# One-core attention and gated FFN: the second exponential path as three shifted linear terms, and the FFN's gate kept in SBUF

## The chip, the cores and the metric

One core of a Trainium2 chip runs the whole program. TensorE multiplies, ScalarE evaluates exp and tanh, VectorE and GpSimd do elementwise work, SyncE issues most transfers. The time is the device time of one execution in microseconds (us); the median of the runs counts, and less is better.

## The reference

Layer norm of one sequence of 2048 tokens of width 512, then two branches on the normed tokens: attention with 32 query heads of width 16 that share one key and one value head, and a gated FFN of width 1792. The FFN's result, through a silu, scales the attention's result, and the input is added.

```python
xn = _layernorm(x, axis=-1)
q = (xn @ wq).reshape(B, S, 32, 16).transpose(0, 2, 1, 3)
k, v = xn @ wk, xn @ wv
p = _softmax(jnp.einsum("bhqd,bkd->bhqk", q, k) * 16 ** -0.5, axis=-1)
s = jnp.einsum("bhqk,bkd->bhqd", p, v).transpose(0, 2, 1, 3).reshape(B, S, 512) @ wo
b = (_silu(xn @ w_gate) * (xn @ w_up)) @ w_down
return x + s * _silu(b)
```

## The kernel before, in words

**Score tiles.** There are 1024 score tiles of 128 keys x 1024 columns (two heads x 512 queries). A block is four heads x 512 queries; it has 16 key tiles with two score tiles each, and there are 32 blocks. A score tile is two matmuls of 32 rows (L877) into one of three PSUM buffers: `ring0` and `ring1` belong to ScalarE, `ring2` to VectorE.

**Two ways to an exponential.** ScalarE reads a tile from `ring0` or `ring1` and writes exp as bf16 into one of eight buffers `Pb` (L937; the first few go to the space of `g2_sb`, shown as `g_sb`). VectorE takes the other tiles, two at a time: for each, one instruction (L997, "pass A") adds an offset to the scaled score, limits it and writes it as a 16-bit integer, whose bits, read as fp16, are a piecewise linear 2 to the power of the score. Over the pair of tiles (2048 columns) three more instructions follow: L1011 cuts out the mantissa, L1016 multiplies it with the value, and L1023 keeps the exponent. The exponent alone and the product are two terms; each is multiplied on TensorE with the value matrix scaled by its own coefficient (`VD[:, i]`), and the sum is the approximated exp times the values. All products add up in `o_ps` (L747).

**FFN.** Its 56 units (`g_ffn`) and 16 down products (`g_down`) fill TensorE's gaps. A unit multiplies the gate into `m_ps`, ScalarE takes tanh of it there (L657), VectorE makes `ab` = (tanh + 1) x gate from `th` and `m_ps` (L659), then the up product goes into the same `m_ps`, and VectorE writes `hT` = `ab` x up (L663). `m_ps` is one buffer: the up product waits for L659, the next unit for L663.

**Order.** A greedy planner in the kernel (`_Sched`, `pe_pick`, `pe_do`, `pump`) places every operation on its engine with costs written in the kernel, and the program is written out in that order; each engine then runs its own list in order. TensorE's list alternates between a *visit* to the scores (row strips: one ScalarE tile, with or without a VectorE tile behind it) and a few *groups* (four matmuls on the four column strips: products with values, FFN, projections). Where the planner sees a gap, it puts a group with zero weights (`zw`) into it. The numbers `TOL` and `MERGE` say how long TensorE may be late for, or wait for, a tile. `LOCKS` names the VectorE operations that the planner does not put beside a GpSimd operation.

Of the kernel before, what the change touches and what calls it, by code (L numbers as in the profile page):

```python
# [26 lines left out]
CE, CW = 0.66858732, 0.66372796  # L27
# [8 lines left out]
TOL, MERGE, KE, KB, KR, PW = 0.17, 0.1, 1000, 3.0, 16, 2.0  # L36
# [146 lines left out]
class _Sched:  # L183
# [4 lines left out]
    LOCKS = ("dM", "dE", "dW", "xn")  # L188
# [95 lines left out]
def kernel(  # L284
# [353 lines left out]
    def g_q(pair):
        qs, jj = pair // NQ, pair % NQ
        a = grp_pe([lambda kc=kc: cmm(m_ps, wq_sb[:, kc, jj * P:(jj + 1) * P], xnT[:, kc, qs * 512:(qs + 1) * 512],  # L640
                                      kc == 0, kc == KC - 1) for kc in range(KC)])
# [4 lines left out]

    cnt = {"f": 0}

    def g_ffn(sc, f):
# [50 lines left out]
    def g_out(n):  # L700
# [280 lines left out]
    w_ops = []  # L981

    def pool_ok(b):
        pend = sum(o.dur for o in w_ops if o.start is None)
        return cur["np"] % KE == 0 and (b > cur["ba"] or rem(b, 0) + rem(b, 1) >= KR) and max(sd.free["POOL"] - sd.free["PE"], 0.0) + pend < KB

    def dve_sc(si, b, x, start, dur):
# [27 lines left out]
        def mul(eng, a, z):  # L1015
            return lambda: eng.tensor_tensor(out=Bf[wi][:, a:z].bitcast(FP16), in0=Bf[wi][:, a:z].bitcast(FP16),  # L1016
                                             in1=U[:, a:z].bitcast(FP16), op=ALU.mult)
        if pool_ok(b):
# [390 lines left out]
```

## Time and profile before

| | |
|---|---|
| median of 3 runs | 781.51 us (780.82 to 781.6) |
| profiled execution, its span | 778.8 us |
| TensorE matmul busy | 748.9 us (96%) |
| VectorE busy | 734.0 us (94%) |
| ScalarE busy | 756.9 us (97%) |
| GpSimd busy | 54.2 us (7%) |
| granted TensorE clock, mean of the core | 0.995 |

Busy time counts an engine from the start to the end of each instruction; an instruction's end overlaps the start of the next one, so the distance from start to start, which the timeline shows, is what one costs in a row of them. The page gives the profiled execution by its span alone; the runs' median lies 2.7 us above it, which is time outside the first and last instruction.

### The profile page before, as it was taken

To read this page: it belongs to the slowest core of one execution; us is meant where nothing else is said; L and a number is where in the kernel's file an instruction comes from. 1 tells how busy PE (TensorE), PEld (TensorE's weight loads), DVE (VectorE), ACT (ScalarE), POOL (GpSimd) and SP (SyncE) were. 2 spreads that over 40 slices of the span, in tenths; PEclk is the share of its full clock that TensorE was granted. 3 is DMA by queue.
4 is the path that set the end of the run, shared out by engine and by line. 5 is a ranking of instruction groups with operands and counts; after the bars stand their busy time and mean duration, and the time that the engine had idled before them with its cause. 6 is when DMAs were issued, how large, how long until landed. Compare 5 with 4: busy or idle time off the path is not lost.

```text
span 778.8 us, 20698 instructions
## 1 busy us (share of the span) xinstructions
PE 748.9 (96%) x9093; PEld 229.7 (29%) x9095; DVE 734.0 (94%) x920; ACT 756.9 (97%) x866; POOL 54.2 (7%) x59
## 2 busy tenths in 40 slices
PE   8999999999999999999999999999999999999995
PEld 3323223322222333322233322322223233322221
DVE  7689999999999999999999999999999999999995
ACT  6999999999999999999999999999999999999993
POOL 2100000000012000000001110000000300000101
PEclk9999999999999999999999999999999999999998
DMA  9400000000001000000000100000000000000001
GB/s 327 141 9 9 16 2 24 3 8 17 4 28 50 23 2 6 18 2 24 2 10 22 49 24 2 24 1 9 16 2 24 28 23 2 2 23 3 22 2 32
DMA packets 21193, 20.15 MB, mean 26 GB/s; under 512 B 8744, under 2 KB 17192, under 8 KB 21096
## 3 DMA queue, kind: packets, MB, share of 16 engines
q1 hardware_dynamic: 19512, 18.20, 7.7%
q8 instruction: 73, 1.20, 0.6%
q10 hardware_dynamic: 1584, 0.56, 0.3%
q14 instruction: 24, 0.20, 0.1%
HBM read 14.19 MB, written 2.34 MB: 21 GB/s over the span
## 4 chain that ended last, share of the span: by engine, by line
PE 48%; ACT 45%; DVE 5%; issue 1%; SPq 0%; DMA 0%; ACTq 0%; POOL 0%; DVEq 0%; POOLq 0%
ACT Pb L937 41%; PE ring L877 17%; PE m_ps L488 16%; PE o_ps L747 13%; ACT th L657 3%; DVE Bf L997 1%; ACT g_sb L937 1%; PE ring L433 1%; DVE Bf L1016 1%; ACT th L674 1%; DVE x_sb L997 0%; DVE Bf L1023 0%; PE ring L488 0%; DVE x_sb L1016 0%; PE ring L452 0%
## 5 line engine op out<-in xcount | busy, mean ns | idle before, releaser
L937 ACT ACTIVATE Pb<-ring 128x1024 bf16<-128x1024 f32 x772 | 730.7, 1202 | 2.1 <-PE ring L877 2.1
L877 PE MATMUL ring<-QB,KT 32*128 32x512 bf16 x2048 | 306.0, 382 | 15.6 <-ACT Pb L937 9.3
L997 DVE TENSOR_SCALAR Bf<-ring 128x1024 uint16<-128x1024 f32 x172 | 209.2, 1216 | 5.2 <-PE ring L877 3.7
L877 PEld LDWEIGHTS <-KT 32*128 32x128 bf16 x2048 | 94.1, 90 | 313.9 <-issue 307.4
L747 PE MATMUL o_ps<-Pb,VA 128*32 128x512 bf16 x1544 | 146.9, 385 | 0.0
L997 DVE TENSOR_SCALAR x_sb<-ring 128x1024 uint16<-128x1024 f32 x72 | 87.6, 1217 | 2.7 <-PE ring L877 2.4
L1016 DVE TENSOR_TENSOR Bf<-Bf,Bf 128x2048 f16<-128x2048 f16 x74 | 90.0, 1216 | 0.1
L747 PE MATMUL o_ps<-xnT,zw 128*32 128x512 bf16 x1092 | 83.1, 381 | 0.0
L488 PE MATMUL m_ps<-xnT,wu_sb 128*32 128x512 bf16 x896 | 72.6, 384 | 1.1 <-DVE ab L659 1.1
L488 PE MATMUL m_ps<-wd_sb,hT 128*32 128x512 bf16 x896 | 71.5, 383 | 0.1
L488 PE MATMUL m_ps<-xnT,wg_sb 128*32 128x512 bf16 x896 | 70.4, 384 | 0.0
L747 PE MATMUL o_ps<-Bf,VD 128*32 128x512 f16 x688 | 67.1, 385 | 0.4 <-DVE Bf L1016 0.3
L732 POOL TENSOR_TENSOR oT<-oa,rb 128x512 bf16<-128x512 f32 x15 | 22.7, 1514 | 614.2 <-DMA rb<-dscr 515.7
L1023 DVE TENSOR_SCALAR Bf<-Bf 128x2048 uint16<-128x2048 uint16 x86 | 60.4, 702 | 0.6
L747 PEld LDWEIGHTS <-VA 128*32 128x32 bf16 x1560 | 38.0, 94 | 53.8 <-issue 51.5
L1011 DVE TENSOR_SCALAR Bf<-Bf 128x2048 uint16<-128x2048 uint16 x74 | 52.1, 712 | 0.0
L657 ACT ACTIVATE th<-m_ps 128x512 f32<-128x512 f32 x56 | 43.7, 781 | 0.0
L659 DVE SCALAR_TENSOR_TENSOR ab<-th,m_ps 128x512 f32<-128x512 f32 x56 | 38.1, 680 | 4.2 <-ACT th L657 3.9
L663 DVE TENSOR_TENSOR hT<-ab,m_ps 128x512 bf16<-128x512 f32 x56 | 38.1, 680 | 2.1 <-PE m_ps L488 1.7
L747 PEld LDWEIGHTS <-VD 128*32 128x32 f16 x976 | 26.6, 94 | 38.9 <-issue 35.3
L747 PEld LDWEIGHTS <-zw 128*32 128x32 bf16 x1092 | 25.8, 95 | 25.5 <-issue 12.9
L1016 DVE TENSOR_TENSOR x_sb<-x_sb 128x2048 f16<-128x2048 f16 x24 | 29.2, 1215 | 0.0
(121 smaller groups left out, 414.3 us busy)
## 6 DMA issues: line engine op xcount, KB each, us to landing
rb<-dscr SPq DMA_DIRECT2D x15, 256.0 KB
out_dram<-xn SPq DMA_DIRECT2D x16, 128.0 KB, 1.9
dn<-oa SPq DMA_DIRECT2D x120, 2.0 KB, 1.7
oa<-oa SPq DMA_DIRECT2D x60, 32.0 KB, 2.0
wg_sb<-in_B_w_gate_dram SPq DMA_DIRECT2D x1, 1792.0 KB, 12.3
wu_sb<-in_B_w_up_dram SPq DMA_DIRECT2D x1, 1792.0 KB
wd_sb<-in_B_w_down_dram SPq DMA_DIRECT2D x1, 1792.0 KB, 19.7
x_sb<-in_A_x_dram SPq DMA_DIRECT2D x3, 512.0 KB
```

The source lines that it names most:

```text
L488: return [nc.tensor.matmul(out=dst[GRP * j:GRP * j + GRP, :], lhsT=w[:, GRP * j:GRP * j + GRP], rhs=rhs, start=start, stop=stop, tile_posi ...
L657: t_ = OP("ACT", 0.477, [a], lambda: nc.scalar.activation(out=th[i][:], in_=m_ps[:], func=ACT.Tanh, scale=0.5), (0,), name="tanh")
L659: s_ = OP("DVE", 0.6, [t_, ab_rel[i]], lambda: nc.vector.scalar_tensor_tensor(out=ab[i][:], in0=th[i][:], scalar=1.0, in1=m_ps[:], op0=ALU ...
L663: h = OP("DVE", 0.6, [b], lambda: nc.vector.tensor_tensor(out=hT[:, f, :], in0=ab[i][:], in1=m_ps[:], op=ALU.mult), (1,), name="hmul")
L732: return [pk, q], lambda eng: eng.tensor_tensor(out=oT[qs % 2][:, jj, :], in0=o0[:], in1=rbt[:], op=ALU.mult)
L747: r.append(nc.tensor.matmul(out=o_ps[GRP * g:GRP * g + GRP, :], lhsT=lhs, rhs=rhs, start=(n == 0), stop=(n == pv_total[(b, g)] - 1), tile_ ...
L877: return lambda: [nc.tensor.matmul(out=ring[sl][:, u * 512:(u + 1) * 512], lhsT=KT[half][GRP * g:GRP * g + GRP, t * P:(t + 1) * P], rhs=QB ...
L937: bi = nc.scalar.activation(out=buf, in_=ring[i][:], func=ACT.Exp, scale=escale, bias=ebias)
L997: lambda: nc.vector.tensor_scalar(out=U[:, hs], in0=ring[si][:], scalar1=ubias, scalar2=UINF, op0=ALU.add, op1=ALU.min), (1.5, u), name="p ...
L1011: o1 = OP("DVE", 0.6, [pa, pa0] + wrel, lambda: nc.vector.tensor_scalar(out=Bf[wi], in0=U, scalar1=0x3FF, scalar2=0x3800, op0=ALU.bitwise_and,
L1016: return lambda: eng.tensor_tensor(out=Bf[wi][:, a:z].bitcast(FP16), in0=Bf[wi][:, a:z].bitcast(FP16), in1=U[:, a:z].bitcast(FP16), op=ALU ...
L1023: o2 = OP("DVE", 0.6, o3, lambda: nc.vector.tensor_scalar(out=U, in0=U, scalar1=0x7C00, scalar2=None, op0=ALU.bitwise_and), (2, u, 1), nam ...
```

## The change

**VectorE's path.** The split into mantissa, product and exponent is gone. The pair's integer itself is the first term; two instructions (L1020 of the changed kernel) add 683 and 341 to it and give the second and the third. Three terms with three coefficients are multiplied with the values on TensorE, and a pair takes three of the ten 2048-column buffers (it took two).

**FFN.** VectorE copies the gate from `m_ps` to `ab` (L665), ScalarE takes tanh from `ab` (L666), so the up product waits for the copy alone; VectorE makes `th` = (tanh + 1) x up (L670), and GpSimd the last product `hT` = `ab` x `th` (L673). There are two `th` buffers (one before). `hT` also takes over the space of `wk_rep` and `o_tok`, and late in the program four tiles of the input are loaded into it.

**The planner.** `MERGE` goes from 0.1 to 0.25, `LOCKS` names the shifts, and the means to give the mantissa product to GpSimd (which `KE` had switched off) go.

```diff
-CE, CW = 0.66858732, 0.66372796
+NPH = 3
+CS = (0.320556640625, 0.2021484375, 0.25439453125)
+SHIFT = (0.0, 683.0, 341.0)
...
-TOL, MERGE, KE, KB, KR, PW = 0.17, 0.1, 1000, 3.0, 16, 2.0
+TOL, MERGE = 0.17, 0.25
...
-    LOCKS = ("dM", "dE", "dW", "xn")
+    LOCKS = ("dS", "xn")
...
-        t_ = OP("ACT", 0.477, [a], lambda: nc.scalar.activation(out=th[i][:], in_=m_ps[:], func=ACT.Tanh, scale=0.5),
-                (0,), name="tanh")
-        s_ = OP("DVE", 0.6, [t_, ab_rel[i]], lambda: nc.vector.scalar_tensor_tensor(
-            out=ab[i][:], in0=th[i][:], scalar=1.0, in1=m_ps[:], op0=ALU.add, op1=ALU.mult), (1,), name="silu")
-        m_rel[0] = s_
+        s_ = OP("DVE", 0.6, [a, ab_rel[i]], lambda: nc.vector.tensor_copy(out=ab[i][:], in_=m_ps[:]), (1,), name="gev")
+        t_ = OP("ACT", 0.477, [s_, th_rel[i]], lambda: nc.scalar.activation(out=th[i][:], in_=ab[i][:], func=ACT.Tanh,
+                                                                            scale=0.5), (0,), name="tanh")
+        m_rel[:] = [s_]
         b = grp_pe([mm(wu_sb, kc) for kc in range(KC)], [ffn_in2])
-        h = OP("DVE", 0.6, [b], lambda: nc.vector.tensor_tensor(
-            out=hT[:, f, :], in0=ab[i][:], in1=m_ps[:], op=ALU.mult), (1,), name="hmul")
-        ab_rel[i] = h
-        m_rel[0] = h
+        u_ = OP("DVE", 0.6, [t_, b], lambda: nc.vector.scalar_tensor_tensor(
+            out=th[i][:], in0=th[i][:], scalar=1.0, in1=m_ps[:], op0=ALU.add, op1=ALU.mult), (1,), name="umul")
+        m_rel[:] = [u_]
+        h = OP("POOL", 1.25, [u_, s_] + hT_use(sc, f), lambda: nc.gpsimd.tensor_tensor(
+            out=hT[:, f, :], in0=ab[i][:], in1=th[i][:], op=ALU.mult), (0,), name="hmul")
+        ab_rel[i] = th_rel[i] = h
+        h_done[f] = h
...
-        o1 = OP("DVE", 0.6, [pa, pa0] + wrel, lambda: nc.vector.tensor_scalar(
-            out=Bf[wi], in0=U, scalar1=0x3FF, scalar2=0x3800, op0=ALU.bitwise_and,
-            op1=ALU.bitwise_or), (2, u, 0), name="dM")
...
-            o3 = [OP("DVE", 1.135, [o1], mul(nc.vector, 0, 2048), (2, u, 2), name="dW")]
-        o2 = OP("DVE", 0.6, o3, lambda: nc.vector.tensor_scalar(
-            out=U, in0=U, scalar1=0x7C00, scalar2=None, op0=ALU.bitwise_and), (2, u, 1), name="dE")
-        for bi, ops, vi in ((ui, [o2], 0), (wi, o3, 1)):
+        terms, rd = [(ui, [pa, pa0], 0)], []
+        for i in range(1, NPH):
+            wi, wrel = get_buf()
+            o = OP("DVE", 0.6, [pa, pa0] + wrel, lambda wi=wi, i=i: nc.vector.tensor_scalar(
+                out=Bf[wi], in0=U, scalar1=SHIFT[i], scalar2=None, op0=ALU.add), (2, u, i), name="dS")
+            rd.append(o)
+            terms.append((wi, [o], i))
+        for bi, ops, vi in terms:
```

What the planner makes of it, counted in the two built programs (for TensorE from the first to the last score tile):

| | before | changed |
|---|---|---|
| score tiles to ScalarE (exp) | 780 | 736 |
| score tiles to VectorE (pass A) | 244 | 288 |
| shifts and the like on 128x2048 | 122 L1011, 122 L1016, 122 L1023 | 288 L1020 |
| TensorE visits to the scores | 772 | 728 |
| TensorE groups of four, of them with zero weights | 1703, 270 | 1677, 85 |
| GpSimd FFN products | 0 | 56 |

In both programs every VectorE tile stands in a visit behind a ScalarE tile.

VectorE's list in the first quarter of the program, before: `Bf` and `x_sb` are the 2048-column buffers, `ring_98` is `ring2`, `m_ps` holds the FFN's gate or up product.

```order
L997 TENSOR_SCALAR x_sb<-ring_98 128x1024
L1016 TENSOR_TENSOR Bf_134<-Bf_134,Bf_133 128x2048
L642 TENSOR_SCALAR QB_120<-m_ps 128x512
L997 TENSOR_SCALAR x_sb<-ring_98 128x1024
L1023 TENSOR_SCALAR Bf_133<-Bf_133 128x2048
L1011 TENSOR_SCALAR x_sb<-Bf_135 128x2048
L997 TENSOR_SCALAR Bf_130<-ring_98 128x1024
L659 SCALAR_TENSOR_TENSOR ab_137<-th_136,m_ps 128x512
L1016 TENSOR_TENSOR x_sb<-x_sb,Bf_135 128x2048
L997 TENSOR_SCALAR Bf_130<-ring_98 128x1024
L663 TENSOR_TENSOR hT<-ab_137,m_ps 128x512
L1023 TENSOR_SCALAR Bf_135<-Bf_135 128x2048
```

About the same place of the changed program: a pass A each, and the shifts, the gate's copy and the product with tanh between them.

```order
L665 COPY ab_136<-m_ps 128x512
L1004 TENSOR_SCALAR x_sb<-ring_98 128x1024
L1020 TENSOR_SCALAR Bf_131<-Bf_129 128x2048
L1020 TENSOR_SCALAR Bf_133<-Bf_129 128x2048
L670 SCALAR_TENSOR_TENSOR th_134<-th_134,m_ps 128x512
L1004 TENSOR_SCALAR Bf_130<-ring_98 128x1024
L1020 TENSOR_SCALAR x_sb<-Bf_132 128x2048
L645 TENSOR_SCALAR QB_119<-m_ps 128x512
L1004 TENSOR_SCALAR Bf_130<-ring_98 128x1024
L1020 TENSOR_SCALAR x_sb<-Bf_132 128x2048
```

Between two passes A there stood one long and one or two short instructions; now there is one or two short ones. Behind each L670 comes a pass A or a shift: of the 56, 32 have a pass A next and 22 a shift.

GpSimd's list of the changed program, in the second FFN stretch: `oT` is the normed attention (L745, before L732) and `xn` the finished output (L708, before L695), which stood there alone before.

```order
L673 TENSOR_TENSOR hT<-ab_136,th_134 128x512
L745 TENSOR_TENSOR oT_143<-oa_140,rb_142 128x512
L673 TENSOR_TENSOR hT<-ab_137,th_135 128x512
L708 TENSOR_TENSOR xn_114<-ab_136,xn_114 128x512
L708 TENSOR_TENSOR xn_115<-ab_137,xn_115 128x512
L708 TENSOR_TENSOR xn_116<-ab_136,xn_116 128x512
L673 TENSOR_TENSOR hT<-ab_137,th_135 128x512
```

To those 27 or so come 56 FFN products, in the four stretches in which the FFN's units run.

## Rows read from the trace of the kernel before

**Rows 1.** The page: busy time, share, instructions; granted clock in 40 slices.
```profile
PE 748.9 (96%) x9093; PEld 229.7 (29%) x9095; DVE 734.0 (94%) x920; ACT 756.9 (97%) x866; POOL 54.2 (7%) x59
...
PEclk9999999999999999999999999999999999999998
```

**Rows 2.** Busy time by stretch: us, PE, PEld, DVE, ACT, POOL, PEclk, DMA share, GB/s.
```profile
12.80:764.20 751.40, 733.54 (x8976) 222.74 (x8981) 719.74 (x875) 749.74 (x851) 47.56 (x42) 1.00 0.07 21
```

**Rows 3.** The page: the chain that ended last, share of the span.
```profile
PE 48%; ACT 45%; DVE 5%; issue 1%; SPq 0%; DMA 0%; ACTq 0%; POOL 0%; DVEq 0%; POOLq 0%
```

**Rows 4.** Timeline of ScalarE: start, length, instruction, count.
```profile
12.83 7.44 ACT L937 ACTIVATE Pb<-ring 128x1024 bf16<-128x1024 f32 x8 [0.48 <-PE ring L877]
...
307.85 0.83 ACT L657 ACTIVATE th<-m_ps 128x512 f32<-128x512 f32 x1
308.32 9.52 ACT L937 ACTIVATE Pb<-ring 128x1024 bf16<-128x1024 f32 x10
...
759.69 5.77 ACT L937 ACTIVATE Pb<-ring 128x1024 bf16<-128x1024 f32 x6
```

**Rows 5.** Groups by line: shapes, count | busy us, mean ns | idle before, releaser.
```profile
L937 ACT ACTIVATE Pb<-ring 128x1024 bf16<-128x1024 f32 x772 | 730.7, 1202 | 2.1 <-PE ring L877 2.1
L997 DVE TENSOR_SCALAR Bf<-ring 128x1024 uint16<-128x1024 f32 x172 | 209.2, 1216 | 5.2 <-PE ring L877 3.7
L1016 DVE TENSOR_TENSOR Bf<-Bf,Bf 128x2048 f16<-128x2048 f16 x74 | 90.0, 1216 | 0.1
L1023 DVE TENSOR_SCALAR Bf<-Bf 128x2048 uint16<-128x2048 uint16 x86 | 60.4, 702 | 0.6
L1011 DVE TENSOR_SCALAR Bf<-Bf 128x2048 uint16<-128x2048 uint16 x74 | 52.1, 712 | 0.0
L657 ACT ACTIVATE th<-m_ps 128x512 f32<-128x512 f32 x56 | 43.7, 781 | 0.0
L663 DVE TENSOR_TENSOR hT<-ab,m_ps 128x512 bf16<-128x512 f32 x56 | 38.1, 680 | 2.1 <-PE m_ps L488 1.7
L659 DVE SCALAR_TENSOR_TENSOR ab<-th,m_ps 128x512 f32<-128x512 f32 x56 | 38.1, 680 | 4.2 <-ACT th L657 3.9
L732 POOL TENSOR_TENSOR oT<-oa,rb 128x512 bf16<-128x512 f32 x15 | 22.7, 1514 | 614.2 <-DMA rb<-dscr 515.7 <-PE m_ps L488 53.1 <-DVE Bf L1023 45.4
L760 DVE COPY oa<-o_ps 128x512 f32<-128x512 f32 (+1 forms) x33 | 22.1, 671 | 5.1 <-PE o_ps L747 4.5
L447 DVE TENSOR_SCALAR xn<-x_sb,mv,rstd 128x512 bf16<-128x512 bf16 x16 | 5.6, 404 | 1.2 <-POOL rstd L444 1.1
```

**Rows 6.** Timeline of TensorE near the end.
```profile
760.13 0.39 PE L877 MATMUL ring<-QB,KT 32*128 32x512 bf16 x2
760.45 0.40 PE L747 MATMUL o_ps<-Pb,VA 128*32 128x512 bf16 x4
760.67 0.39 PE L488 MATMUL ring<-wo_sb,oT 128*32 128x512 bf16 x4
761.00 0.39 PE L877 MATMUL ring<-QB,KT 32*128 32x512 bf16 x2
```

**Rows 7.** Timeline of VectorE near the end.
```profile
756.81 1.23 DVE L997 TENSOR_SCALAR Bf<-ring 128x1024 uint16<-128x1024 f32 x1
757.95 0.68 DVE L1023 TENSOR_SCALAR Bf<-Bf 128x2048 uint16<-128x2048 uint16 x1
758.55 0.69 DVE L1011 TENSOR_SCALAR Bf<-Bf 128x2048 uint16<-128x2048 uint16 x1
```

**Rows 8.** Timelines of GpSimd and VectorE at two GpSimd products.
```profile
426.81 1.16 POOL L695 TENSOR_TENSOR xn<-ab,xn 128x512 bf16<-128x512 f32 x1 [1.27 <-DVE ab L690]
427.78 0.74 DVE L1011 TENSOR_SCALAR x_sb<-x_sb 128x2048 uint16<-128x2048 uint16 x1
...
556.78 1.57 POOL L732 TENSOR_TENSOR oT<-oa,rb 128x512 bf16<-128x512 f32 x1 [48.34 <-DMA rb<-dscr]
557.13 1.77 DVE L1011 TENSOR_SCALAR Bf<-Bf 128x2048 uint16<-128x2048 uint16 x1
```

More of the change, by code (lines that the diff above doesn't have):

```diff
@@ L586, in pro_v @@
         vs = []
-        for i in (-1, 0, 1):
+        for i in range(-1, NPH):
             d = [OP("POOL", 0.33, d, lambda i=i: e_vbuild(c, i), (0,), name="vb")]
@@ L623 @@
     d_gate = [brel["2a"], brel["2b"], brel["m"]]
-    buf_rel = [[] for _ in range(7)] + [xn_done[0], xn_done[1], xn_done[2]]
+    buf_rel = [[] for _ in range(6)] + [xn_done[c] for c in range(4)]
     buf_seq = [0] * len(buf_rel)
@@ L632, in grp_pe @@
         for emit in parts:
-            last = OP("PE", MMF, [m_rel[0], last] + list(deps), emit, (2,), "c", "fill")
+            last = OP("PE", MMF, m_rel + [last] + list(deps), emit, (2,), "c", "fill")
             m_open[id(last)] = True
@@ L643, in g_q, with hT_use @@
                                                                 scalar2=None, op0=ALU.mult), (1,), name="qev")
-        m_rel[0] = e
+        m_rel[:] = [e]
         q_ready[pair] = [e]
     cnt = {"f": 0}
+    th_rel, h_done, hT_rd = [None] * 2, {}, [None]
+    def hT_use(sc, f):
+        return [hT_rd[0][1]] if hT_rd[0] is not None and hT_rd[0][0] == sc - 1 else []
+    hT_last = [None]
     def g_ffn(sc, f):
@@ L670, in g_down @@
         a = grp_pe([lambda f=f: cmm(m_ps[:, :D], hT[:, f, tt * P:(tt + 1) * P], wd_sb[:, f, :], f == 0, f == FC - 1)
-                    for f in range(FC)])
+                    for f in range(FC)], [h_done[f] for f in range(FC)])
+        hT_last[0] = a
+        hT_rd[0] = (sc, a)
         i = cnt["f"] % 2
         cnt["f"] += 1
-        t_ = OP("ACT", 0.477, [a], lambda: nc.scalar.activation(out=th[i][:, :D], in_=m_ps[:, :D], func=ACT.Tanh,
+        t_ = OP("ACT", 0.477, [a, th_rel[i]], lambda: nc.scalar.activation(out=th[i][:, :D], in_=m_ps[:, :D], func=ACT.Tanh,
                                                                 scale=0.25), (0,), name="tanh2")
@@ L678, in g_down @@
             (1,), name="g2")
-        m_rel[0] = s_
+        m_rel[:] = [s_]
+        th_rel[i] = s_
         g_ready[n] = s_
@@ L794, in dve_key @@
     def dve_key(o):
-        if o.name in ("dM", "dE", "dW") and pair_blk[o.prio[1]] < cur["ba"]:
+        if o.name == "dS" and pair_blk[o.prio[1]] < cur["ba"]:
             return (0.9,) + o.prio[1:]
@@ L979, in get_buf @@
         return i, rel
[L981 to L985, printed above, removed]
     def dve_sc(si, b, x, start, dur):
@@ L1068, in g_h0 @@
         for qq in range(4):
-            a = OP("PE", 0.25, [m_rel[0], a, oev[LB - 1]], lambda qq=qq: tq_emit(0, [qq], m_ps[:, qq * P:(qq + 1) * P]),
+            a = OP("PE", 0.25, m_rel + [a, oev[LB - 1]], lambda qq=qq: tq_emit(0, [qq], m_ps[:, qq * P:(qq + 1) * P]),
                    (2,), "f", "fill")
-        m_rel[0] = OP("DVE", 0.8, [a], lambda: tq_norm(0, range(4), m_ps[:]), (1,), name="h0")
+        m_rel[:] = [OP("DVE", 0.8, [a], lambda: tq_norm(0, range(4), m_ps[:]), (1,), name="h0")]
     def g_checks():
@@ L1102, in pump @@
     def pump(now):
-        r = m_rel[0]
-        if r is not None and r.start is None:
+        if any(r is not None and r.start is None for r in m_rel):
             return
         p = cur["issued"]
+        if job["f"] == len(ffn_list) and not job["xl"]:
+            job["xl"] = True
+            OP("DMA", 2.2, [hT_last[0]], lambda: nc.sync.dma_start(out=hT[:, 4:8, :D], in_=x_v[:, LN:LN + 4, :]), (0,))
         if job["f"] == len(ffn_list) and not job["chk"] and planned([dens_op.get(LB - 2)]):
```

36 lines of the change are left out of this document (14 added, 22 removed).

## The prediction

> **What bounds the kernel now.** I read the page first: three engines are busy for 94 to 97% of the span and the TensorE clock is granted in full but at the very end [rows 1], so the shares alone do not name the bound. The busy time of the stretch in which exps run does: from 12.80 to 764.20 us ScalarE is busy for 749.74 of 751.40 us, TensorE for 733.54, VectorE for 719.74 [rows 2]. ScalarE does not rest; TensorE's figure holds zero-weight work as well. The chain that ended last names TensorE with 48% and ScalarE with 45% [rows 3]: it hops between the two, since each exp waits for its scores and each new score tile for its buffer. So the time is ScalarE's list, plus what it waits for TensorE.
>
> In numbers: the first exp starts at 12.83 and the last of six ends at 759.69 + 5.77 = 765.46 [rows 4]; one lasts 1.20 [rows 5], so the last starts at 764.26. In these 751.4 us lie 779 distances from one exp to the next and 72 tanh. A tanh takes 308.32 - 307.85 = 0.47 to the next start [rows 4]; 72 of them take 33.8. That leaves (751.4 - 33.8) / 779 = 0.921 for an exp, its waits for TensorE included. From the last exp's start to the end of the span are 14.5 us.
>
> **ScalarE.** 780 exps become 736. 735 x 0.921 = 677.0, and 33.8 for tanh: 710.8, against 751.4. With head and tail as before (12.8 and 14.5) the span is 738.1, if every exp still costs its 0.921. Tanh now reads SBUF. No row shows that for fp32; at nothing or at 0.05 each (an estimate, a tenth of its 0.47) it is 0 to 2.8 us, and I take 1.
>
> **TensorE, which must feed it.** Near the end a score visit starts 0.32 before the group behind it, two groups lie 0.22 apart, and the last group 0.33 before the next visit [rows 6]. A visit with k groups is then 0.65 + 0.22 (k - 1). Before: 772 visits with 1703 groups, 763 of which are the first in their run: 772 x 0.65 + 940 x 0.22 = 709. After: 728 visits, 1677 groups, 719 firsts: 728 x 0.65 + 958 x 0.22 = 684. TensorE's list thus gets 25 us shorter while ScalarE's gets 40 us shorter. And what is in it differs: the zero groups fall from 270 to 85, so the real work goes from 709 - 59 = 650 to 684 - 19 = 665. It has to fit into 711 instead of 751: from 86 to 94%. The cause is the third term, 432 value groups for VectorE's tiles where there were 244, less 22 for ScalarE's. So TensorE, which could be late now and then without harm, becomes nearly as full as ScalarE.
>
> How much of that comes out as ScalarE waiting? If TensorE keeps all the time it now spends outside its list (751.4 - 709 = 42.4), it needs 684 + 42.4 = 726.4 between first and last exp, 15.6 more than ScalarE's 710.8; if those waits shrink with the work that fills them, nothing. I take the middle, 7.8, since real groups stand where zeros stood but the gaps too short for a group stay. The span is 738.1 + 1 + 7.8 = 746.9.
>
> **VectorE.** A pass A is followed by the next instruction after 757.95 - 756.81 = 1.14, a short one over 2048 columns after 0.60 [rows 7]; the product L1016 lasts as long as a pass A, 1216 ns each [rows 5], so I put 1.14 on it. Before: 244 x 1.14 + 122 x (0.60 + 1.14 + 0.60) = 563.6. After, with 0.60 for a shift: 288 x 1.14 + 288 x 0.60 = 501.1. That is 62.5 us less for 44 tiles more. Adding to a 16-bit integer and writing one back has no row; the two short operations L1011 and L1023 have the same shape and types and differ in being bitwise, at 712 and 702 ns [rows 5]. In the other direction stands L447, arithmetic on 16-bit values: 404 ns for 512 columns, where a quarter of a short one would be 150 (0.60 / 4) [rows 5]; it takes its scalars from memory, the shift has a constant. The ends are 0.60 and 1.14; shape, type and constant speak for 0.60.
>
> In the FFN two VectorE instructions on 512 PSUM columns are exchanged for two others: L659 and L663 at 680 each, the new copy like L760 at 671, the new product like L659 [rows 5]. That is nothing. The up product no longer waits for tanh: VectorE waited 3.9 us for it in all [rows 5], which is the most that this can give, and I give it nothing. Of what is new in the queues, the first down product in each of the four FFN stretches waits for GpSimd's last product, some 1.5 us behind L670, where it waited for nothing but VectorE. Value groups and score visits stand in TensorE's list in between; without that cover it would be 6 us. The load of input into `hT` is one more entry in SyncE's list (146 rows, before 145), after the last down product, and its reader is in the tail; I put nothing on it.
>
> **GpSimd and VectorE side by side.** 56 products like L732 (1514 ns in the mean [rows 5]; its like takes 1.16 undisturbed [rows 8]) come to GpSimd, some 80 us of work on an engine that is busy for 54. GpSimd's time is free, but VectorE's beside it is not. At 556.78 GpSimd starts a product; the L1011 that starts at 557.13 takes 1.77 instead of 0.68, to the moment at which GpSimd ends (558.35) and its own work after it. At 426.81 a pass A lies beside GpSimd, and the L1011 behind it takes 0.74 [rows 8]. So a short VectorE instruction beside a GpSimd product costs from 0.06 to 1.09 more: 56 times that is 3 to 61 us. The Trainium skill says this outright (SBUF — State Buffer, "Who interferes with whom"): VectorE in its two-port modes and GpSimd exclude each other for a whole instruction, "the other fully blocks". The rows agree. Taken at its worst it speaks against this change: each of the 56 products would hold a shift for its whole length, and the gain on VectorE would be gone. By the order 32 of the 56 have a pass A behind L670, which does not wait at 426.81; I take 0.3 each, 17 us, out of the 62.5 that came free. VectorE then stands at 734.0 - 62.5 + 17 = 688.5 of 747, 92% against 94%, and is not the bound.
>
> **The larger MERGE.** TensorE may now wait up to 0.25 us, not 0.1, at a VectorE tile behind a ScalarE tile. All 244 already stood there, so there is no visit to be saved by it; what it buys is more tiles, which the counts hold already. What it costs is 0 to 0.15 for each of 288: 0 to 43 us, behind which the groups of that visit and the next ScalarE tile queue. It is hidden as long as ScalarE's two buffers hold work; I put it into the 7.8 above and its end into the range.
>
> **Sum.** 746.9 for the span against 778.8 before, that is 32 us less; with the 2.7 us that lie between span and median, 749.6. I forecast 750.
>
> **Rivals.**
> - *ScalarE alone sets the time:* its waits stay as they are, 738 to 741 for the span, 742 us as time. For it: waits before are short (2.1 us idle before L937 in all, [rows 5]). Against: TensorE's 94%. Chance 0.30.
> - *TensorE sets it:* its 42.4 stay, span 738.1 + 15.6 + 1 = 754.7, time 757. With MERGE's waits at 0.05 for each tile (14 us more) 772. Chance 0.25, of which 0.05 beyond 766.
> - *GpSimd blocks VectorE in full:* VectorE needs 734.0 - 62.5 + 61 = 732.5; at the 94% it reaches now that is a span of 777 and a time of 780, no change. This is the rule of the page above as a mechanism of this kernel. For it the 1.77, against it the 0.74 and the order. It begins to bind at (0.94 x 747 - 671.5) / 56 = 0.55 per product. Chance 0.04.
> - *The shifts run at half rate* (this one ends slower): 288 x 0.54 = 155.5 more on VectorE, 671.5 + 155.5 = 827, at 94% a span of 880, time 880. It decides from 0.82 us per shift on: (734.0 - 671.5) / 288 = 0.22 over 0.60. For it L447, against it L1011 and L1023. Chance 0.04. The Trainium skill gives `tensor_scalar` on 16-bit data in SBUF its highest rate, 693 ns for 2048 columns (VectorE: DVE Perf Modes, "The perf-mode tier table"); by it this rival falls, L1011 and L1023 agree with it and L447 does not.
>
> My own forecast, between the first two, has 0.37.
>
> **Range and chances.** 740 to 766 holds the forecast, nine tenths of the first rival and all but a fifth of the second, about 0.37 + 0.27 + 0.20 = 0.84. The likeliest case alone is 744 to 756. The 0.04 of the blocked VectorE part into 0.01 faster, 0.02 no change, 0.01 slower. Faster by over 0.2%: 0.37 + 0.30 + 0.25 + 0.01 = 0.93. Within 0.2% (about what a measurement of this kernel can tell from no change): 0.02. Slower: 0.04 from the shifts and 0.01, 0.05.
>
> **What would show it.** After: 736 exps at 0.92 to 0.94 from start to start; L1020 at about 0.70 in the mean, with some of 1 to 1.8 beside GpSimd; VectorE's share falling by a little, GpSimd's rising to some 130 us; idle time before L950 (exp) by TensorE of some 10 us where there were 2.1. I am wrong if a shift lasts over 0.9 in the mean, if exps lie more than 0.95 apart, or if TensorE's waits for `ring2` come to tens of us.

## The result, and the profile after

The changed kernel takes 745.26 us in the median of 4 runs (744.46 to 745.66), the kernel before 781.48 (780.82 to 781.6): a ratio of 0.9537, 95% interval 0.9524 to 0.955. The forecast was 750 with 740 to 766. The profiled execution took 744.99 us, with a span of 743.1.

The page of the changed kernel: busy time, granted clock in 40 slices, and the chain by engine, as [rows 1, 3].

```profile
PE 721.5 (97%) x8999; PEld 217.0 (29%) x8999; DVE 682.4 (92%) x886; ACT 718.1 (97%) x822; POOL 127.0 (17%) x120
...
PEclk9999999999999999999999999999999999999998
...
ACT 59%; PE 34%; DVE 4%; issue 2%; POOL 0%; ACTq 0%; DVEq 0%; POOLq 0%
```

ScalarE is as full as before. Its share of the chain that ended last rose from 45 to 59%. VectorE has 682.4 us where 688.5 were forecast, GpSimd 127.0 where 130 were.

ScalarE's timeline at the first exp, around two tanh, and at the last exps, as [rows 4].

```profile
12.87 1.94 ACT L950 ACTIVATE Pb<-ring 128x1024 bf16<-128x1024 f32 x2 [0.48 <-PE ring L890]
...
306.70 0.78 ACT L666 ACTIVATE th<-ab 128x512 f32<-128x512 f32 x1
307.22 5.76 ACT L950 ACTIVATE Pb<-ring 128x1024 bf16<-128x1024 f32 x6
...
719.55 0.67 ACT L686 ACTIVATE th<-m_ps 128x512 f32<-128x512 f32 x1
720.03 8.44 ACT L950 ACTIVATE Pb<-ring 128x1024 bf16<-128x1024 f32 x9
```

From here the sum of the prediction is made again. The last of nine exps ends at 728.47 and lasts 1.18 (group below), so it starts at 727.29. A tanh from SBUF takes 307.22 - 306.70 = 0.52 to the next start, one from PSUM (L686) 0.48 as before; 56 x 0.520 + 16 x 0.477 = 36.8. The 735 distances then take 727.29 - 12.87 - 36.8 = 677.7, which is 0.922 each.

| term of the span, us | forecast | measured |
|---|---|---|
| before the first exp | 12.8 | 12.9 |
| 735 exps at the old 0.921 | 677.0 | 677.7 (0.922) |
| TensorE nearly full | 7.8 | 0.7, the difference in the row above |
| tanh | 33.8 + 1 | 36.8 |
| after the start of the last exp | 14.5 | 15.8 |
| span | 746.9 | 743.1 |
| from the span to the median | 2.7 | 2.2 |

The last row mixes two things: the profiled execution itself took 1.9 us more than its span (744.99 - 743.1), and the rest is its distance from the median of the runs. The same holds for the 2.7 us of before.

Groups of the changed kernel by line, as [rows 5]: count, busy us, mean ns, idle before and releaser.

```profile
L950 ACT ACTIVATE Pb<-ring 128x1024 bf16<-128x1024 f32 x728 | 687.9, 1181 | 3.8 <-PE ring L890 1.9 <-PE o_ps L760 1.8
L950 ACT ACTIVATE g_sb<-ring 128x1024 bf16<-128x1024 f32 x8 | 7.8, 1148 | 0.0
L890 PE MATMUL ring<-QB,KT 32*128 32x512 bf16 x2048 | 291.7, 383 | 7.1 <-ACT Pb L950 3.9 <-ACT g_sb L950 0.3
L1004 DVE TENSOR_SCALAR Bf<-ring 128x1024 uint16<-128x1024 f32 x172 | 209.7, 1219 | 10.9 <-PE ring L890 9.2
...
L673 POOL TENSOR_TENSOR hT<-ab,th 128x512 bf16<-128x512 f32 x56 | 78.2, 1396 | 356.7 <-DVE th L670 356.7
...
L1020 DVE TENSOR_SCALAR Bf<-Bf 128x2048 uint16<-128x2048 uint16 x101 | 72.1, 723 | 0.2
...
L1020 DVE TENSOR_SCALAR Bf<-x_sb 128x2048 uint16<-128x2048 uint16 x74 | 50.8, 694 | 0.3
L1020 DVE TENSOR_SCALAR x_sb<-Bf 128x2048 uint16<-128x2048 uint16 x71 | 50.5, 716 | 0.4
...
L1020 DVE TENSOR_SCALAR x_sb<-x_sb 128x2048 uint16<-128x2048 uint16 x42 | 29.5, 703 | 0.1
```

The shift runs like the bitwise operations L1011 and L1023 [rows 5]; the rival of half rate is gone. All 736 exps (728 and 8 that write `g_sb`) wait 3.8 us for others; some 10 had been forecast from TensorE alone. VectorE waits 9.2 us for scores in its largest group, against 3.7 before [rows 5]: VectorE now stands ready before its scores more often than it did.

### The profile page after: what moved, and what is told of

It reads as the page before. It is cut to its first block, busy times and chain, and to the rows that moved or that the text cites. A ratio compares the mean times of both kernels' runs of the same rounds, so it can differ in the third digit from the quotient of the medians.

```text
span 743.1 us, 20569 instructions
## 1 busy us (share of the span) xinstructions
PE 721.5 (97%) x8999; PEld 217.0 (29%) x8999; DVE 682.4 (92%) x886; ACT 718.1 (97%) x822; POOL 127.0 (17%) x120
## 3 DMA queue, kind: packets, MB, share of 16 engines
q8 instruction: 72, 1.18, 0.7%
## 4 chain that ended last, share of the span: by engine, by line
ACT 59%; PE 34%; DVE 4%; issue 2%; POOL 0%; ACTq 0%; DVEq 0%; POOLq 0%
ACT Pb L950 54%; PE ring L890 12%; PE o_ps L760 12%; PE m_ps L491 9%; ACT th L666 3%; ACT g_sb L950 1%; DVE Bf L1020 1%; DVE Bf L1004 1%; ACT th L686 1%; DVE x_sb L1020 1%; DVE x_sb L1004 1%; PE ring L491 0%; DVE ab L665 0%; PE ring L455 0%; DVE xn L708 0%
## 5 line engine op out<-in xcount | busy, mean ns | idle before, releaser
L950 ACT ACTIVATE Pb<-ring 128x1024 bf16<-128x1024 f32 x728 | 687.9, 1181 | 3.8 <-PE ring L890 1.9
L1004 DVE TENSOR_SCALAR x_sb<-ring 128x1024 uint16<-128x1024 f32 x116 | 141.5, 1220 | 7.6 <-PE ring L890 5.8
L673 POOL TENSOR_TENSOR hT<-ab,th 128x512 bf16<-128x512 f32 x56 | 78.2, 1396 | 356.7 <-DVE th L670 356.7
L1020 DVE TENSOR_SCALAR Bf<-Bf 128x2048 uint16<-128x2048 uint16 x101 | 72.1, 723 | 0.2
L760 PE MATMUL o_ps<-x_sb,VD 128*32 128x512 f16 x684 | 64.1, 384 | 0.0
L760 PEld LDWEIGHTS <-VA 128*32 128x32 bf16 x1472 | 36.8, 94 | 54.2 <-issue 50.6
L1020 DVE TENSOR_SCALAR Bf<-x_sb 128x2048 uint16<-128x2048 uint16 x74 | 50.8, 694 | 0.3
L1020 DVE TENSOR_SCALAR x_sb<-Bf 128x2048 uint16<-128x2048 uint16 x71 | 50.5, 716 | 0.4
L745 POOL TENSOR_TENSOR oT<-oa,rb 128x512 bf16<-128x512 f32 x15 | 19.7, 1313 | 162.8 <-DMA rb<-dscr 153.0
L665 DVE COPY ab<-m_ps 128x512 f32<-128x512 f32 x56 | 38.3, 685 | 6.8 <-PE m_ps L491 6.4
L666 ACT ACTIVATE th<-ab 128x512 f32<-128x512 f32 x56 | 43.7, 781 | 0.0
L670 DVE SCALAR_TENSOR_TENSOR th<-th,m_ps 128x512 f32<-128x512 f32 x56 | 38.2, 682 | 4.0 <-PE m_ps L491 3.4
L1020 DVE TENSOR_SCALAR x_sb<-x_sb 128x2048 uint16<-128x2048 uint16 x42 | 29.5, 703 | 0.1
```

Of the source, the lines that this page charges most:

```text
L665: s_ = OP("DVE", 0.6, [a, ab_rel[i]], lambda: nc.vector.tensor_copy(out=ab[i][:], in_=m_ps[:]), (1,), name="gev")
L666: t_ = OP("ACT", 0.477, [s_, th_rel[i]], lambda: nc.scalar.activation(out=th[i][:], in_=ab[i][:], func=ACT.Tanh, scale=0.5), (0,), name="t ...
L670: u_ = OP("DVE", 0.6, [t_, b], lambda: nc.vector.scalar_tensor_tensor(out=th[i][:], in0=th[i][:], scalar=1.0, in1=m_ps[:], op0=ALU.add, op ...
L673: h = OP("POOL", 1.25, [u_, s_] + hT_use(sc, f), lambda: nc.gpsimd.tensor_tensor(out=hT[:, f, :], in0=ab[i][:], in1=th[i][:], op=ALU.mult) ...
L745: return [pk, q], lambda eng: eng.tensor_tensor(out=oT[qs % 2][:, jj, :], in0=o0[:], in1=rbt[:], op=ALU.mult)
L760: r.append(nc.tensor.matmul(out=o_ps[GRP * g:GRP * g + GRP, :], lhsT=lhs, rhs=rhs, start=(n == 0), stop=(n == pv_total[(b, g)] - 1), tile_ ...
```

## The experiments

Two theories stood at the start: that ScalarE's list alone sets the pace (Theory 1), and that TensorE, nearly full, costs ScalarE time (Theory 2); a third gives the FFN's new form a part of its own. Every run is worked out as above: first and last exp start, less the tanh between them (0.52 from SBUF, 0.477 from PSUM), gives the distance of an exp; from the last exp's start to the span's end is the tail. "Late" counts FFN groups of four that stand behind the last score tile in the built program. The distance and the tail come from the one profiled execution of a kernel, the time is the median of its runs; e5's profiled execution (763.5 us) is 4 us shorter than its median and e7's (751.8) 2 us longer. Each edit also lets the planner write a new order for the whole program, so no run differs from the changed kernel in the named lines alone.

| kernel | exps | late | us for an exp | tail, us | time, us | ratio to before |
|---|---|---|---|---|---|---|
| before | 780 | 0 | 0.920 | 14.6 | 781.5 | |
| changed | 736 | 0 | 0.922 | 15.8 | 745.3 | 0.9537 [0.9524, 0.9550] |
| e1 MERGE 0.1 | 758 | 0 | 0.924 | 14.6 | 767.2 | 0.9822 [0.9805, 0.9838] |
| e2 old FFN | 730 | 116 | 0.928 | 78.0 | 800.3 | 1.0255 [1.0230, 1.0279] |
| e3 new FFN alone | 784 | 0 | 0.928 | 15.4 | 792.9 | 1.0132 [1.0106, 1.0158] |
| e4 extra groups | 730 | 120 | 0.931 | 67.2 | 792.1 | 1.0140 [1.0123, 1.0157] |
| e5 tanh from `m_ps` | 738 | 0 | 0.949 | 15.3 | 767.4 | 0.9826 [0.9810, 0.9843] |
| e6 last product on VectorE | 748 | 0 | 0.926 | 14.4 | 757.5 | 0.9687 [0.9667, 0.9707] |
| e7 two terms | 734 | 0 | 0.935 | 15.3 | 749.7 | 0.9586 [0.9565, 0.9607] |
| e8 two terms, MERGE 0.6 | 710 | 0 | 0.923 | 18.0 | 722.7 | 0.9244 [0.9228, 0.9259] |
| e9 e7, reciprocal later | 734 | 0 | 0.917 | 15.2 | 739.1 | 0.9457 [0.9441, 0.9472] |
| e10 MERGE 0.6 | 730 | 42 | 0.937 | 32.8 | 765.5 | 0.9790 [0.9766, 0.9814] |
| e11 before, MERGE 0.25 | 780 | 0 | 0.924 | 15.7 | 784.0 | 1.0029 [1.0017, 1.0042] |
| e12 up behind tanh | 742 | 0 | 0.921 | 18.4 | 752.5 | 0.9627 [0.9611, 0.9643] |

**e1: the changed kernel with the old MERGE.**

```diff
-TOL, MERGE = 0.17, 0.25
+TOL, MERGE = 0.17, 0.1
```

> The changed kernel with MERGE back at 0.1; the planner then gives ScalarE 758 exps (736 in the changed kernel). Theory 1 (ScalarE's list sets the time, 0.922 us for an exp with its waits, TensorE's fuller list costs nothing): 745.3 + 22 x 0.922 = 765.5 us. Theory 2 (TensorE sets the time as well, and its waits at VectorE's tiles cost): those waits go, and the real groups on TensorE fall by 17, so at most half of that loss: 745 to 756 us.

767.2 us, as Theory 1 had it: 22 of the 44 exps that the change takes from ScalarE come from MERGE, at nearly the same distance of an exp (0.924). What is left of the change without them is worth 14 us.

**e2: the three terms with the old FFN.** `th` is written from `m_ps`, `ab` = (tanh + 1) x gate and `hT` are made on VectorE as before; MERGE is 0.25.

```diff
-        s_ = OP("DVE", 0.6, [a, ab_rel[i]], lambda: nc.vector.tensor_copy(out=ab[i][:], in_=m_ps[:]), (1,), name="gev")
+        t_ = OP("ACT", 0.477, [a, th_rel[i]], lambda: nc.scalar.activation(out=th[i][:], in_=m_ps[:], func=ACT.Tanh, scale=0.5),
+                (0,), name="tanh")
+        s_ = OP("DVE", 0.6, [t_, ab_rel[i]], lambda: nc.vector.scalar_tensor_tensor(
+            out=ab[i][:], in0=th[i][:], scalar=1.0, in1=m_ps[:], op0=ALU.add, op1=ALU.mult), (1,), name="silu")
...
+        h = OP("DVE", 0.6, [b], lambda: nc.vector.tensor_tensor(
+            out=hT[:, f, :], in0=ab[i][:], in1=m_ps[:], op=ALU.mult), (1,), name="hmul")
```

> The changed kernel with the FFN as before (tanh from PSUM, both FFN products on VectorE, none on GpSimd), the three terms and MERGE 0.25 kept; 730 exps. Theory 1: 745.3 - 6 x 0.922 - 56 x 0.043 (tanh back to 0.477) = 737.3 us, faster than the changed kernel, so that the FFN's part of the change gains nothing. Theory 3 (taking tanh out of the wait of the up product and a product off VectorE is where the gain comes from): over 755 us.

800.3 us, 19 more than before the change and 55 more than with the new FFN. Theory 1 falls. The loss does not show as waits for exps (0.928) but behind them. ScalarE's timeline at the end of e2, and the busy time of that stretch (columns as in [rows 2]):

```profile
716.83 3.08 ACT L949 ACTIVATE Pb<-ring 128x1024 bf16<-128x1024 f32 x3
721.66 0.60 ACT L665 ACTIVATE th<-m_ps 128x512 f32<-128x512 f32 x1 [1.75 <-PE m_ps L491]
726.01 0.60 ACT L665 ACTIVATE th<-m_ps 128x512 f32<-128x512 f32 x1 [3.75 <-PE m_ps L491]
731.21 0.60 ACT L665 ACTIVATE th<-m_ps 128x512 f32<-128x512 f32 x1 [4.60 <-PE m_ps L491]
737.26 0.60 ACT L665 ACTIVATE th<-m_ps 128x512 f32<-128x512 f32 x1 [5.45 <-PE m_ps L491]
743.31 0.60 ACT L665 ACTIVATE th<-m_ps 128x512 f32<-128x512 f32 x1 [5.46 <-PE m_ps L491]
```

```profile
719.00:796.60 77.60, 44.30 (x536) 18.16 (x528) 23.04 (x47) 8.22 (x14) 2.69 (x2) 0.74 0.05 15
```

The exps are over at 720; 116 FFN groups are not. Each unit now runs alone through `m_ps` (gate, tanh, `ab`, up, `hT`), up to 6.05 us from tanh to tanh, while ScalarE is busy for 8 of 78 us and the mean granted clock is 0.74.

Part of the 55 us belongs to MERGE, which stayed at 0.25 here. With the three terms, the old FFN and MERGE 0.1 the built program has 752 exps and 46 late groups; it was not run. An estimate from the runs, 745.3 + 16 x 0.922 - 2.4 + 46 x 0.53 (a late group's 62 / 116 us in e2), is 782 us: no gain over the kernel before, but 15 us behind e1 and not 55.

**e3: the new FFN with the old split and MERGE 0.1.** All edits of the FFN and of the buffers stay; mantissa, product and exponent are back, and `LOCKS` names them again.

> The changed kernel with VectorE's path as before (mantissa, product, exponent; two terms) and MERGE 0.1; the FFN stays changed. 784 exps. Theory 1: 745.3 + 48 x 0.922 = 789.6 us, slower than the kernel before (781.5). Theory 3: 755 to 770 us.

792.9 us, 11 more than the kernel before, as Theory 1 had it (789.6); Theory 3's 755 to 770 is missed. Alone the FFN's new form gains nothing: VectorE has no more room than before, 784 exps remain (780 before), at 0.928 each, and 56 tanh read SBUF. So neither half of the change gained alone as it was run, the terms with MERGE 0.25 and the FFN with 0.1.

**e4: 147 more groups with zero weights**, one behind each pair of VectorE tiles, in the changed kernel.

```diff
+        xg = OP("PE", MMF, [oev[b - 1], pv], pv_emit(b, [(zw[:], xnT[:, 0, 0:512], g) for g in range(4)]),
+                (1, b, cur["nA"]), "c", "dpv")
+        blk_pv[b].append(xg)
```

> The changed kernel with one more group of four matmuls with zero weights for every pair of VectorE's tiles, which adds nothing to the sums; 730 exps, 147 such groups, real and added groups together 1619 + 2 where there were 1592, the planner's own zero groups 65 (85). Theory 1: TensorE still has room, 745.3 - 6 x 0.922 = 739.8 us, at most 744. Theory 2: 147 x 0.22 = 32 us more that TensorE must do, of which the 20 zero groups fewer give back 4: 755 to 773 us.

792.1 us, beyond what either theory gave. Exps lie 0.931 apart, some 7 us over all of them; the rest is again a tail, of 120 FFN groups:

```profile
740.70 0.63 ACT L666 ACTIVATE th<-ab 128x512 f32<-128x512 f32 x1 [3.18 <-DVE ab L665]
744.51 0.63 ACT L666 ACTIVATE th<-ab 128x512 f32<-128x512 f32 x1 [3.18 <-DVE ab L665]
748.32 0.63 ACT L666 ACTIVATE th<-ab 128x512 f32<-128x512 f32 x1 [3.18 <-DVE ab L665]
```

With the new FFN a unit that runs alone takes 3.81 us.

**Theory 4**, formed from these: as long as exps run, ScalarE's list sets the pace at 0.92 to 0.93 an exp; want of room on TensorE or in `m_ps` appears as FFN left over, which runs alone at the end.

**e5: tanh reads `m_ps`**, the rest of the new FFN stays.

```diff
-        t_ = OP("ACT", 0.477, [s_, th_rel[i]], lambda: nc.scalar.activation(out=th[i][:], in_=ab[i][:], func=ACT.Tanh,
+        t_ = OP("ACT", 0.477, [a, th_rel[i]], lambda: nc.scalar.activation(out=th[i][:], in_=m_ps[:], func=ACT.Tanh,
...
-        m_rel[:] = [s_]
+        m_rel[:] = [s_, t_]
```

> The changed kernel, but tanh reads the gate in m_ps as it did before, and the up product waits for the copy and for tanh; the rest of the new FFN stays (gate copied, last product on GpSimd). 738 exps; no FFN group stands behind the last score tile in the order. Theory 4 (the exps' rhythm times their number, plus the FFN that is left over at the end): nothing is left over, so 745.3 + 2 x 0.92 for two more exps - 2.4 for tanh from PSUM (72 - 16 = 56 of them at 0.043 less) = 744.7 us. Rival (that the up product need not wait for tanh is what the new FFN is worth): each of 56 units keeps m_ps 0.8 us or more longer, FFN is left over again, over 755 us.

767.4 us: Theory 4 missed by 23 us, the rival held in size. Nothing is left over; the exps lie 0.949 apart. Two waits of e5 that the changed kernel does not show (us in total, times, longest):

```profile
ACT th L666 <- DVE ab L665: 7.1, 18, 2.5
...
DVE ab L665 <- ACT th L666: 6.2, 12, 0.7
```

Copy and tanh, two readers of one PSUM buffer, wait for each other in the built program: in none of the 56 units do they overlap in the trace, and in 46 the second starts 32 to 35 ns after the first has ended. From the start of an exp to the start of the tanh behind it are 1.146 us in the mean of 56, against 0.914 in the changed kernel: 13 us, of which one wait alone is 2.5. Exp to exp is 0.932 against 0.923, 6 us more. That is what the profiled execution is longer (its span is 761.7 against 743.1); the 4 us more of the median lie outside this trace.

**e12: the other half of e5.** Tanh reads the copy, but the planner places the up product behind tanh.

```diff
-        m_rel[:] = [s_]
+        m_rel[:] = [s_, t_]
```

> The changed kernel, tanh from the copied gate, but the planner places the up product behind tanh, as if it needed m_ps until then. 742 exps; no FFN group stands behind the last score tile. Theory 4: 745.3 + 6 x 0.922 = 750.8 us; the 22 us of the run with tanh from m_ps then come from the two readers of m_ps, copy and tanh, that took turns there. Rival (they come from the later up product alone): 765 us or more.

752.5 us, 1.7 above Theory 4, with 742 exps at 0.921 and a tail 2.6 longer. So the 13 and 6 us of e5 come with the two readers of `m_ps`, which e12 does not have. The later place of the up product costs 7 us in e12, 5.5 of them as six more exps; e5, with 738 exps, does not pay this in the same way.

**e6: the last FFN product on VectorE.**

```diff
-        h = OP("POOL", 1.25, [u_, s_] + hT_use(sc, f), lambda: nc.gpsimd.tensor_tensor(
+        h = OP("DVE", 0.6, [u_, s_] + hT_use(sc, f), lambda: nc.vector.tensor_tensor(
...
-    LOCKS = ("dS", "xn")
+    LOCKS = ("dS", "xn", "hmul")
```

> The changed kernel, but the FFN's last product hT runs on VectorE and not on GpSimd. 748 exps (VectorE has less room, so 12 score tiles more go to ScalarE); no FFN group stands behind the last score tile. Theory 4: 745.3 + 12 x 0.922 = 756.4 us. Rival (GpSimd's products hold up VectorE and so cost time in the changed kernel): without them VectorE's waits go, 745 us or less in spite of the 12 exps.

757.5 us. GpSimd's product is worth 12 exps, some 12 us; what it takes from VectorE by standing beside it is less.

**e7: two terms.**

```diff
-NPH = 3
-CS = (0.320556640625, 0.2021484375, 0.25439453125)
-SHIFT = (0.0, 683.0, 341.0)
+NPH = 2
+CS = (0.4806, 0.33984)
+SHIFT = (0.0, 512.0)
```

> The changed kernel with two shifted terms (shifts 0 and 512) instead of three, MERGE still 0.25. It approximates the exp more coarsely than the changed kernel. 734 exps, VectorE has one shift less for each pair, TensorE 138 groups less of real work (174 zero groups in their place and fewer groups in all). Theory 4: TensorE's room is worth nothing while exps run, 745.3 - 2 x 0.922 = 743.5 us. Rival (TensorE, at 94% real work, costs ScalarE time, as the prediction's 7.8 us had it): exps come closer together, 738 us or less.

749.7 us, 4.5 more than the changed kernel with less work on VectorE and on TensorE. Neither theory had that. Timelines of e7 for VectorE, TensorE and ScalarE around one place, and the stretch by 2 us:

```profile
568.90 0.35 DVE L734 RECIPROCAL rc<-dn 128x32 f32<-128x32 f32 x1 [3.69 <-DMA dn<-oa]
569.17 1.16 DVE L1004 TENSOR_SCALAR x_sb<-ring 128x1024 uint16<-128x1024 f32 x1
...
568.06 0.39 PE L890 MATMUL ring<-QB,KT 32*128 32x512 bf16 x2
570.38 0.39 PE L890 MATMUL ring<-QB,KT 32*128 32x512 bf16 x2 [1.94 <-DVE x_sb L1004]
...
562.92 6.85 ACT L950 ACTIVATE Pb<-ring 128x1024 bf16<-128x1024 f32 x7
572.25 1.02 ACT L950 ACTIVATE Pb<-ring 128x1024 bf16<-128x1024 f32 x1 [2.48 <-PE ring L890]
```

```profile
568.00:570.00 2.00, 0.45 (x6) 0.10 (x3) 1.10 (x2) 1.77 (x2) 0.00 (x0) 1.00 0.15 33
570.00:572.00 2.00, 1.62 (x12) 0.31 (x11) 1.97 (x3) 0.00 (x0) 0.00 (x0) 0.71 0.13 25
572.00:574.00 2.00, 2.00 (x16) 0.38 (x18) 0.79 (x2) 1.26 (x2) 0.00 (x0) 0.50 0.35 113
```

The reciprocal stands at the head of VectorE's list before its denominators have landed, and holds it for 3.69 us. Behind it a pass A is late, its buffer `ring2` stays taken, TensorE waits 1.94 us for the buffer, and behind that are the scores of ScalarE, which waits 2.48. In the stretch in which TensorE is busy for 0.45 of 2 us nothing happens to the clock yet; in the two that follow it is 0.71 and 0.50 (the 1.2 GHz level). The waits of VectorE at the reciprocal in e7, in the changed kernel and in e1 (us in total, times, longest), and what the exps of e7 wait for:

```profile
DVE rc L734 <- DMA dn<-oa: 14.5, 11, 3.7
...
DVE rc L734 <- DMA dn<-oa: 1.6, 3, 0.8
...
DVE rc L734 <- DMA dn<-oa: 11.5, 10, 2.6
...
L950 ACT ACTIVATE Pb<-ring 128x1024 bf16<-128x1024 f32 x726 | 686.7, 1171 | 10.6 <-PE ring L890 10.1
```

The sum of these waits is not what counts: e1 has nearly as much of them as e7, and its exps wait for only 4.4 us and lie 0.924 apart. Of e7's waits at the reciprocal the three longest (2.2, 3.2 and 3.7 us) are each followed by a wait of ScalarE of 1.4 to 2.5 us. Of its 10 us of waits for exps some 7 stand within 8 us behind a reciprocal that waited; the others do not.

**e9: e7 with the reciprocal later.** The planner's figure for the denominators' transfer goes up.

```diff
-        dens_op[b] = OP("DMA", 2.4, [ev], dens, (0,))
+        dens_op[b] = OP("DMA", 5.0, [ev], dens, (0,))
```

> The two-term kernel with MERGE 0.25 of two runs before, but the planner is told that the transfer of the denominators takes 5.0 us after its tile's copy and not 2.4, so it places the reciprocal (L734) later in VectorE's list. 734 exps as there. Theory 5 (the 6 us that the two-term kernel lost against 0.922 for each exp are VectorE's waits at the reciprocal, 14.5 us in 11 places, behind which pass A, TensorE and then ScalarE stood): those waits fall below 4 us, and the time to 743.5 us. Rival (two terms themselves make exps lie further apart): 748 us or more.

739.1 us: 10.6 us less than e7 from the one figure, which places 15 reciprocals later and moves what stands around them; more than the 6 that were sought. No reciprocal waits for a transfer any more. The exps of e9 and what they wait for:

```profile
L950 ACT ACTIVATE Pb<-ring 128x1024 bf16<-128x1024 f32 x726 | 687.2, 1215 | 1.3 <-PE ring L890 1.3
```

1.3 us of waits where e7 had 10.6 and the changed kernel 3.8; 0.917 an exp against 0.922. The 733 x 5 ns = 3.7 us are the most that this shows for TensorE's fuller list in the changed kernel, since e9 has 139 groups of real work fewer. The later reciprocal was not tried in the changed kernel itself.

**e8: two terms and MERGE 0.6.**

> Two shifted terms as in the run before it, and MERGE at 0.6 instead of 0.25: TensorE may wait up to 0.6 us for VectorE's one slot behind a ScalarE tile. The exp is approximated more coarsely, as there. 710 exps, 314 VectorE tiles; no FFN group stands behind the last score tile. Theory 4: 745.3 - 26 x 0.922 = 721.3 us. Rival (waits of TensorE for the slot come out as waits for exps): 314 waits of 0.1 and more beyond what ScalarE's buffers cover, 740 us or more.

722.7 us, a ratio of 0.9244 to before, 22.5 us under the changed kernel: the fastest of all. A larger MERGE gives VectorE 24 tiles more than e7, and their waits do not reach ScalarE. It holds for the coarser exp of e7; e8 with e9's edit was not run.

**e10: MERGE 0.6 with three terms.**

> The changed kernel (three terms) with MERGE 0.6 instead of 0.25. 730 exps; 42 FFN groups stand behind the last score tile in the order. Theory 4: six exps less give 745.3 - 6 x 0.922 = 739.8, but the 42 groups run alone at the end, at the 62 us that 116 of them added to the tail of the kernel with the old FFN (0.53 each) 22 us: 762 us. Rival (a larger MERGE is only gain): 740 us.

765.5 us, 3.5 above Theory 4. The tail grew by 17 us (forecast 22), and exps lie 0.937 apart, 11 us more. With three terms TensorE has no room for the waits that MERGE allows: FFN is left over.

**e11: the kernel before with MERGE 0.25.**

```diff
-TOL, MERGE, KE, KB, KR, PW = 0.17, 0.1, 1000, 3.0, 16, 2.0
+TOL, MERGE, KE, KB, KR, PW = 0.17, 0.25, 1000, 3.0, 16, 2.0
```

> The kernel before, with MERGE 0.25 instead of 0.1 and nothing else. 780 exps and 244 VectorE tiles, as with 0.1; 772 visits. Theory 4 (MERGE only pays where VectorE has room for more tiles; before, it had none): 781.5 us, no change. Rival (a larger MERGE by itself gives the 22 us that it gives in the changed kernel): 760 us.

784.0 us, the same 780 exps, 0.3% slower. A larger MERGE gave VectorE more tiles only in the runs with the shorter VectorE path.

## Why the prediction was right, and where it was off

- **The bound.** ScalarE's list plus its waits: right. The distance of an exp was 0.920 before and 0.922 after, and between 0.917 and 0.937 in all runs but e5 (0.949).
- **TensorE nearly full, 7.8 us:** mis-sized. It was between 0.7 (the table of terms) and 3.7 (e9). Of the two ends in the prediction the lower came true: the time TensorE spent outside its list fell from 42.4 to 714.4 - 684 = 30.4 us. So the runs bear out the mechanism of the first rival, ScalarE alone (742 us), and not the middle that I took; 745.3 lies nearer to that rival than to 750, and what it lies above it is tanh and the tail. What the prediction did not have is where TensorE's want of room goes when there is more of it: into a tail (62, 51 and 17 us more in e2, e4 and e10) far more than into waits (exps 0.928 to 0.937 apart there).
- **The FFN on VectorE, "I give it nothing":** this step failed, though it changed no number of the sum. It looked for the gain in VectorE's waits (3.9 us). The counts of the built program, on which the sum rests, held the gain already: without the FFN's new form the same shorter program leaves 116 groups behind the last exp, 55 us at MERGE 0.25 (e2). With tanh kept on `m_ps` it is 22 us (e5, by the two readers of `m_ps`), with the up product placed behind tanh 7 (e12), without GpSimd 12 (e6).
- **Tanh from SBUF, 1 us:** 2.4, from 56 x 0.043; within the bounds of 0 to 2.8. The Trainium skill (VectorE: DVE Perf Modes, "The TRN2 errata — SBUF-src ops pay a fixed extra latency per instruction") gives ScalarE 224 cycles and the columns from SBUF, 172 from PSUM, at 1.2 GHz: an estimate of 43 ns more from that page, which the 0.520 and 0.477 of this trace agree with.
- **The tail, 14.5:** 15.8. The 1.3 us were not followed up.
- **GpSimd beside VectorE, 17 us:** mis-sized, and without effect on the sum. One form of the shift in the changed kernel (shortest, median, longest ns), and one place at which a shift stands beside GpSimd:

```profile
L1020 DVE TENSOR_SCALAR Bf<-Bf x101: 629/684/1768, 48.8 to 722.6; 128x2048 uint16<-128x2048 uint16 x101
```

```profile
431.75 0.69 DVE L1020 TENSOR_SCALAR x_sb<-Bf 128x2048 uint16<-128x2048 uint16 x1
432.35 1.77 DVE L1020 TENSOR_SCALAR Bf<-Bf 128x2048 uint16<-128x2048 uint16 x1
...
432.26 1.31 POOL L745 TENSOR_TENSOR oT<-oa,rb 128x512 bf16<-128x512 f32 x1 [3.25 <-DMA rb<-dscr]
```

  The four groups of L1020 are busy for 202.9 us; 288 at the median of 0.684 are 197.0. So the shifts lost 6 us, not 17. VectorE's busy time came out only 6.1 us under the forecast and not 11, so some 5 us of its other work were missed, and what they are was not looked for. The Trainium skill's rule of the full block (SBUF — State Buffer, "Who interferes with whom") is seen at 432.35: GpSimd's product ends at 433.57, the shift at 434.12, which is about its own work later. 26 shifts in all last 0.79 us or more; each stands beside a GpSimd product and ends 0.55 us after it. But 22 of them last 0.99 or less, since in 24 of the 26 a pass A stands directly in front, and only the end of GpSimd's product is left for the shift.
- **The larger MERGE:** "what it buys is more tiles, which the counts hold already" was right, and is 22 us of the 36 (e1). Its cost of up to 43 us did not come in the changed kernel; at 0.6 some of it did, 11 us on the exps (e10).

What stays open: why copy and tanh take turns at `m_ps` in e5. The releasers come from semaphores, so the turns stand in the built program, though the planner asks for none between the two; whether the two reads could run together was not tried.

## What to carry to other kernels

Where a planner fills gaps, a shortage on a second engine need not appear as waits of the bounding one: count what of the filler work stands behind the last instruction of the bounding engine, since it runs there alone, at the latency of its chain (up to 6.05 us a unit with the old FFN, 3.81 with the new one here) and not at its busy time. A parameter that lets one engine wait (MERGE) is worth what the freed engine can take: 22 us with the shorter VectorE path and the new FFN, nothing in the kernel before. And look at the head of every list for an instruction that waits for a transfer: a reciprocal of 0.35 us held VectorE for up to 3.69 us, and a planner's figure of 5.0 in place of 2.4 us, which moved it back, gave 10.6 us in the kernel with two terms.

## What the runs showed that I had not expected

- A stop of TensorE of 1.94 us, itself the end of a chain that began at a DMA, was followed by two stretches of 2 us at 0.71 and 0.50 of the clock (e7); the wait of ScalarE (2.48 us) was longer than the one of TensorE that caused it.
- Two engines that read the same PSUM buffer took turns in all 56 units (e5), though neither writes it, and ScalarE lost 13 us by it.
- With less work for VectorE and TensorE the kernel became slower (e7 against the changed one): VectorE, with more room, stood longer at its waits for transfers (14.5 us against 1.6), and with these gone the kernel was the faster one (e9).
